# Attention and two feed-forward layers on one core: in the second pass, ready weight parts from DRAM, sums in place, and the next group's first unit ahead of each second stage

## The chip, the core and the metric

The kernel runs on one core of a Trainium2 chip. The metric is the device time of one execution in microseconds; the time before is the median of three runs, 1068.46 us (1065.6 to 1068.74).

## What is computed

Causal attention with a recurrent memory over 4 x 8 heads of 576 tokens and width 64; then two gated feed-forward layers on 2304 tokens of width 512. All of it is float32.

```python
...
    g = x @ w_gate
    silu = g * (1.0 / (1.0 + np.exp(-g)))
    val = x @ w_val
    return (silu * val @ w_out).astype(np.float32)
...
    h = x @ w_in
    g = h * (1.0 / (1.0 + np.exp(-1.702 * h)))
    return (g @ w_out).astype(np.float32)
```

The first layer has `d_ff` 1536, the second 2048. The weights come as 64-bit numbers and are decoded on the chip into float32, chunk by chunk (68 chunks of 128 x 512).

## The kernel before, in words

**Precision.** A float32 operand is split into a rounded high part (ScalarE casts it) and the rest as a low part (a subtraction on GpSimd or VectorE). A product is three matmuls: high by high, high by low, low by high.

**First pass.** Attention and both layers for the first 1024 tokens, a group of chunks at a time. Per chunk, `load_w` loads, `dec` decodes (ScalarE, VectorE, GpSimd), `spl0` (L160) and `spl1` (L163) make the two parts in the buffer `wp`, and 24 matmuls `m` of 512 columns use them. For the second pass `keep` (L176) stores the decoded float32 weights of two chunks (a pair) in a DRAM tile: for inner rows (the chunks of a `w_out`) four planes of 128 x 256, for the others seven, the last of them sums that `add_up` (L165) makes on GpSimd.

**Second pass.** The other 1280 tokens. Here each 2 x 2 block product of matrices is done with seven block products and not eight; the blocks are 640 columns wide. The names of the program:

- `P(l,g,k,j)`: product j of 0 to 6 in unit k of group g of layer l, the first stage (into the hidden rows). A unit is seven products; the first layer (l = 0) has three groups of four units, the second (l = 1) four groups of two.
- `Q(l,g,u,j)`: product j of half u in the second stage of a group (back to width 512): fourteen products. Q(l,g) below is such a stage.
- A product is 12 matmuls `c` of 320 columns; there are 238.
- Forms: the seven combinations of data blocks that the products take: `B11`, `B21`, `B22` are blocks, `T1` to `T4` differences of blocks (`t1` to `t4`, VectorE, L1072), each split by `hi` (ScalarE, L1088) and `lo` (L1093, VectorE, a few on GpSimd). For a Q they are made from its group's unit results (`f`), for a layer once from the layer's input (`xh`, `xl`, `th`, `tl`).
- In a unit: `s` copies product 0, `u` = s + product 2, `v` = u + product 3, `c22` = v + product 4, `u4` = u + product 4, `c21` = v + product 6, `c12` = u4 + product 5 (VectorE additions on PSUM, L1039); `tan2`, `gat2` and `mul` are the gate. Product 1 adds onto product 0 in PSUM. In a Q products 1, 5 and 6 do so onto 0, 4 and 3, after the sum `E` (L1110, VectorE) has read the bank.
- `E` adds a product into the output rows or into `csum`; `fin` (L1115) adds `csum` at a layer's end; `put` stores.
- Weights: `raw` (L976) loads a pair's planes, `add` (L984) makes four sums on GpSimd for inner rows, and for each product `wh` (ScalarE, L992) and `wl` (GpSimd, L996) split one plane into a buffer `wb`.

**What sets the order.** `schedule` plays a list schedule with given durations and keys; `pinned` emits each engine's instructions in that order, and an engine works its own list in order. `plan_three` writes the sequence of products: for each group all units, then its Q. Keys for forms come from tables (`SOON`, `THEN`), and tables of numbers (`SHARE`, `LEAD`) shift the first pass.

```python
            if l and g == 0 and WOVEN:
                todo = [(k, j) for j in OPEN for k in ks]
            else:
                todo = [(k, j) for k in ks for j in (LAST if g or not l or k else OPEN)]
...
            qs = [(u, j) for j in (CLOSE if close else SECOND) for u in range(2)]
```

The two units of group 0 of layer 1 are woven: each product of the one, then of the other.

Of the kernel before, what the change touches and what calls it, by code (L numbers as in the profile page):

```python
# [35 lines left out]
def tile_attention_moe_moe(  # L36
# [13 lines left out]
    nc = tc.nc  # L50
# [7 lines left out]
    const = ctx.enter_context(tc.tile_pool(name="const", bufs=1))  # L58
# [55 lines left out]
    kept = {i: dram.tile([128, 7 if first(i) else 4, 256], F32, name=f"w{i}") for i in range(0, NCK, 2)}  # L114
# [61 lines left out]
    def keep(i):  # L176
        a = raws[i].rearrange("p (a n) -> p a n", a=2)
        if not first(i):
            x = i % 2
            nc.sync.dma_start(out=kept[i - x][:, 2 * x:2 * x + 2], in_=a)  # L180
        elif i % 2 == 0:
            nc.sync.dma_start(out=kept[i][:, 0:2], in_=a)
        else:
            nc.sync.dma_start(out=kept[i - 1][:, 2:6], in_=sums.pop(i))
            nc.sync.dma_start(out=kept[i - 1][:, 6], in_=a[:, 1])
# [332 lines left out]
    PACE, DEC, SHARE, LEAD, XKEY = 2.93, 4.02, 0.879, 16.5, 60.16  # L518
# [54 lines left out]
    def decode_ops(ops, i, use, split=True, decode=True):  # L573
# [15 lines left out]
        if i % 2 == 0:
            ops["keep", i] = "SP", 0.4, need + 6.0, (("dec2", i),), (), ()  # L590
            return
        for x in range(2):
            ops["sum", i, x] = "Pool", 1.75, need + 5.0, (("spl1", i),) if x == 0 else (("sum", i, 0),), \
                ("sums",) if x == 0 else (), (("wa", ("dec0", i - 1)),) if x else ()
        ops["keep", i] = "SP", 0.8, need + 8.0, (("sum", i, 1),), (), (
            ("sums", ("sum", i, 0)), ("wa", ("dec0", i)))
# [39 lines left out]
    def plan_one():  # L636
# [12 lines left out]
    LATE = (("B11", 0), ("B22", 0), ("T3", 1), ("T4", 0))  # L649
    EV, WB, RAW = -2.5, 6.7, -10.3  # L650
    SOON = {
        "t1": 1.8, "t3": 5.2, "T3": -69.2, "t2": -31.2, "T2": 9.5, "B11": -15.2, "B21": 5.2, "T1": -15.6, "t4": -17.2,
        "T4": -11.8, "B22": -11.9}
    THEN = {
        "t1": -12.1, "t3": 6.5, "T3": 8.5, "t2": -1.6, "T2": 14.7, "B11": -17.8, "B21": 1.7, "T1": -11.5, "t4": 3.4,
        "T4": 16.0, "B22": 2.5}
    OPEN, CLOSE = (0, 1, 2, 3, 4, 6, 5), (0, 4, 1, 5, 3, 2, 6)
    WOVEN, HEAD = True, 3
# [34 lines left out]
    def form_ops(ops, G, b, key, to_f, from_t, late=(), early=False, wait=()):  # L693

        at_ = SOON if early else THEN

        def op(name, kd, after, takes=(), gives=()):
            ops[(name, G, kd)] = "DVE", 0.82, key + at_[name], tuple(after), takes, gives

        def split(F, kd, after, gives=()):  # L700
            after = (*after, *(wait if F[0] == "B" or F == "T1" else ()))
            ops["hi", G, F, kd] = "Act", 0.68, key + at_[F], after, ("f",) if to_f else (), ()
            e, us = ("Pool", 1.85) if (F, kd) in late else ("DVE", 0.82)
            ops["lo", G, F, kd] = e, us, key + at_[F], (("hi", G, F, kd),), (), tuple(gives)

        for kd in range(2):
# [16 lines left out]

# [3 lines left out]
    def plan_three(ops, t0, ready, gets):  # L727

        seq, n = [], 0
        for l, g in groups():  # L730
            base = 36 + 8 * g if l else 12 * g
            ks = (0, 2) if l else (0, 1, 2, 3)
            if l and g == 0 and WOVEN:
                todo = [(k, j) for j in OPEN for k in ks]
            else:
                todo = [(k, j) for k in ks for j in (LAST if g or not l or k else OPEN)]
            for k, j in todo:
                seq.append(("P", l, g, k, j))
                flat.append((base + (k if l else 2 * k), j))
            close = not l and g == 2  # L740
            qs = [(u, j) for j in (CLOSE if close else SECOND) for u in range(2)]
            if close and HEAD < 7:
                qs = qs[:2 * HEAD] + [(u, j) for u in range(2) for j in CLOSE[HEAD:]]
            for u, j in qs:
                seq.append(("Q", l, g, u, j))
                flat.append((base + (4 if l else 8) + 2 * u, j))
        left = {}
        for m, (i, j) in enumerate(flat):
            left[i] = m
        keys = [t0 + STEP * m for m in range(len(seq))]  # L750
        seen = set()
        for m, (i, j) in enumerate(flat):
            key = keys[m] - WB
            first = seq[m][0] == "P"
            if i not in seen:
                seen.add(i)
                ops["raw", i] = "SP", 2.2, key - RAW, (("seam", 1), *([("raw", was)] if m else gets)), ("raw",), ()
                was = i
                if not first:
                    for x in range(4):  # L760
                        ops["add", i, x] = "Pool", 0.88, key - 1.0, (("add", i, x - 1) if x else ("raw", i),), (), ()
            ops["wh", m] = "Act", 0.42, key, (
                ("raw", i) if first else ("add", i, 3), *([("wh", m - 1)] if m else [])), ("wb",), ()
            ops["wl", m] = "Pool", 0.9, key, (("wh", m),), (), (("raw", ("raw", i)),) if left[i] == m else ()
        start = {}
        for m, n in enumerate(seq):
            key, wb = keys[m], ("wb", ("wh", m))
            if n[0] == "P":
                _, l, g, k, j = n
                U = l, g, k  # L770
                after = [("wl", m), *ready[l][FORMS[j]], *seq[max(m - 1, 0):m]]
                if j == 1:
                    after.append(("s", *U))
                ops[n] = "PE", STEP, key, tuple(after), ("pc",) if j != 1 else (), (wb,)
# [5 lines left out]
                def P(j):  # L780
# [506 lines left out]
```

## Time and profile before

| what | value |
|---|---|
| median of three runs | 1068.46 us |
| the profiled execution | 1066.52 us, its span 1064.7 us |
| TensorE busy | 1004.1 us, 94% of the span |
| VectorE, GpSimd, ScalarE busy | 875.4, 804.4, 596.7 us |
| mean granted TensorE clock | 0.981 |
| data moved by DMA | 119.59 MB |

A row of the timeline is one or more instructions of one line in a row on one engine, with the idle time before them and what ended it. A row of a group gives its count, busy time and mean, and the idle time of the engine just before it. Consecutive matmuls overlap, so their pace is read from start to start, and a busy share of TensorE near 100% can hold slow matmuls. The granted clock is a share of 2.4 GHz.

### The profile page before, as it was taken

Reading aid. Unit: us, or ns where it says so; the run is one execution under the profiler, and the core shown is the slowest. Engines: PE = TensorE matmul, PEld = TensorE weight load, DVE = VectorE, ACT = ScalarE, POOL = GpSimd, SP = SyncE. Lnnn points to the kernel's source line nnn. Section 1 sums busy time; section 2 is a strip of 40 time slices with the busy share of each in tenths; the row PEclk is TensorE's granted clock in tenths of the full one; section 3 lists DMA queues with packets and bytes.
Section 4 is the critical chain, followed back from the end, with each engine's and each line's share of the span. In section 5 each row is a group of like instructions: output and inputs, shape, how many; then the busy total and the mean of one; then the engine's idle time right before and its main releaser. Section 6 shows DMA issues by size and latency. Waiting matters only on the chain.

```text
span 1064.7 us, 16958 instructions
## 1 busy us (share of the span) xinstructions
PE 1004.1 (94%) x5959; PEld 864.9 (81%) x5959; DVE 875.4 (82%) x1180; ACT 596.7 (56%) x1231; POOL 804.4 (76%) x808
## 2 busy tenths in 40 slices
PE   7998998999999999999999999999998689899896
PEld 4665776778787777777888999999997679799895
DVE  8999589777878977686889686697799996969797
ACT  6897466557465666755555455443444465535351
POOL 7879578886877767656564898797797787858685
PEclk9999999999999999999999999999999799999998
DMA  5362446564545434443544211203102103020202
GB/s 173 102 203 74 151 168 192 184 200 155 182 141 171 149 118 143 170 149 120 179 179 153 95 40 70 89 22 104 55 21 70 41 1 109 1 90 21 89 21 99
DMA packets 48932, 119.59 MB, mean 112 GB/s; under 512 B 7632, under 2 KB 14288, under 8 KB 48848
## 3 DMA queue, kind: packets, MB, share of 16 engines
q1 hardware_dynamic: 48704, 118.51, 33.5%
q8 instruction: 47, 0.77, 0.3%
q14 instruction: 37, 0.30, 0.1%
q10 hardware_dynamic: 144, 0.00, 0.0%
HBM read 85.46 MB, written 33.03 MB: 111 GB/s over the span
## 4 chain that ended last, share of the span: by engine, by line
PE 61%; DVE 27%; issue 4%; POOL 3%; ACT 3%; DMA 2%; SPq 0%; POOLq 0%; ACTq 0%; DVEq 0%
PE m L88 27%; PE c L88 24%; DVE t L1072 4%; PE o L88 4%; DVE f L1093 4%; PE s L88 3%; DVE t L1052 3%; DVE t L1039 2%; PE tp L361 2%; DVE acc L1110 2%; DVE nm L310 1%; DVE xl L1093 1%; DVE wa L146 1%; DVE sm L340 1%; DVE csum L1110 1%
## 5 line engine op out<-in xcount | busy, mean ns | idle before, releaser
L996 POOL TENSOR_TENSOR wb<-raw,wb 128x256 fp32r<-128x256 f32 x238 | 218.7, 940 | 62.3 <-ACT wb L992 61.0
L88 PE MATMUL c<-f,wb 128*128 128x320 f32 x1176 | 185.7, 319 | 26.6 <-DVE acc L1110 15.8
L88 PE MATMUL m<-xh,wp 128*128 128x512 f32 x640 | 210.3, 398 | 0.5 <-POOL wp L163 0.5
L88 PEld LDWEIGHTS c<-f,wb 128*128 128x128 f32 x1176 | 180.3, 195 | 31.1 <-DVE acc L1110 18.1
L88 PEld LDWEIGHTS m<-xh,wp 128*128 128x128 f32 x640 | 120.0, 188 | 35.0 <-issue 5.1
L88 PE MATMUL m<-hh,wp 128*128 128x512 f32 x448 | 147.6, 399 | 0.0
L149 POOL TENSOR_TENSOR wa<-wa,wr 128x512 uint32<-128x512 uint32 x68 | 95.7, 1409 | 65.3 <-DVE wa L146 48.3
L992 ACT CAST wb<-raw 128x256 fp32r<-128x256 f32 x238 | 89.6, 403 | 87.0 <-PE c L88 55.8
L163 POOL TENSOR_TENSOR wp<-wa,wp 128x512 fp32r<-128x512 f32 x68 | 95.1, 1398 | 55.8 <-ACT wp L160 55.0
L88 PE MATMUL c<-xh,wb 128*128 128x320 f32 x640 | 132.3, 312 | 4.4 <-ACT xh L1088 4.2
L1039 DVE TENSOR_TENSOR t<-t,c 128x640 f32<-128x640 f32 x120 | 95.4, 814 | 42.3 <-PE c L88 34.8
L88 PE MATMUL m<-xl,wp 128*128 128x512 f32 x320 | 124.7, 390 | 0.0
L1088 ACT CAST f<-t 128x640 fp32r<-128x640 f32 x98 | 71.2, 727 | 86.5 <-DVE t L1072 69.6
L88 PEld LDWEIGHTS c<-xh,wb 128*128 128x128 f32 x640 | 104.6, 191 | 5.1 <-ACT xh L1088 4.5
L88 PEld LDWEIGHTS m<-hh,wp 128*128 128x128 f32 x448 | 84.7, 189 | 21.2 <-issue 3.5
L88 PE MATMUL c<-th,wb 128*128 128x320 f32 x480 | 99.8, 311 | 0.3
L1072 DVE TENSOR_TENSOR t<-t,t 128x640 f32<-128x640 f32 x64 | 87.8, 1385 | 2.4 <-POOL t L1056 2.2
L88 PE MATMUL m<-hl,wp 128*128 128x512 f32 x224 | 87.8, 392 | 0.0
L349 POOL TENSOR_SCALAR p<-p,sm 128x256 f32<-128x256 f32 (+3 forms) x128 | 76.0, 611 | 13.7 <-DVE sm L341 5.2
L1093 DVE TENSOR_TENSOR f<-t,f 128x640 fp32r<-128x640 f32 x70 | 79.1, 1134 | 4.6 <-ACT f L1088 4.2
L88 PEld LDWEIGHTS c<-th,wb 128*128 128x128 f32 x480 | 78.2, 189 | 1.1 <-DVE t L1039 1.1
L88 PE MATMUL c<-xl,wb 128*128 128x320 f32 x320 | 73.9, 313 | 4.1 <-DVE xl L1093 4.1
(128 smaller groups left out, 2096.6 us busy)
## 6 DMA issues: line engine op xcount, KB each, us to landing
w<-w SPq DMA_DIRECT2D x40, 512.0 KB, 3.8
raw<-w SPq DMA_DIRECT2D x20, 896.0 KB, 4.6
w<-wo SPq DMA_DIRECT2D x28, 512.0 KB, 3.5
w<-wa SPq DMA_DIRECT2D x48, 256.0 KB, 3.3
w<-sums SPq DMA_DIRECT2D x20, 512.0 KB, 2.7
qk<-qk SPq DMA_DIRECT2D x32, 288.0 KB, 3.8
raw<-w SPq DMA_DIRECT2D x28, 256.0 KB, 3.0
nq<-nat SPq DMA_DIRECT2D x16, 320.0 KB, 3.8
```

Of the source, the lines that this page charges most:

```text
L88: nc.tensor.matmul(o, w, x, start=start, stop=stop, skip_group_check=more)
L149: nc.gpsimd.tensor_tensor(au, au, r, op=ALU.add)
L163: nc.gpsimd.tensor_sub(parts[i][:, 1], raws[i], f(parts[i][:, 0]))
L349: nc.gpsimd.tensor_scalar(p[:, j, c:c + n], p[:, j, c:c + n], sm[:, x, j:j + 1], 1.0, op0=ALU.mult, op1=ALU.mult)
L992: nc.scalar.copy(wb[:, 0], RAWS[i][:, j])
L996: nc.gpsimd.tensor_sub(WBS[m][:, 1], RAWS[i][:, j], f(WBS[m][:, 0]))
L1039: nc.vector.tensor_add(wide_(t), wide_(TT[(a, *U)]), pc("P", *U, j))
L1052: nc.vector.scalar_tensor_tensor(t, t, 1.0, c_in(n[:3], n[3]), op0=ALU.add, op1=ALU.mult)
L1072: nc.vector.tensor_sub(t, block(G, a, kd), block(G, b, kd))
L1088: nc.scalar.copy(form(G, F, kd)[0], block(G, SRC[F], kd))
L1093: e.tensor_sub(l, block(G, SRC[F], kd), f(h))
L1110: nc.vector.scalar_tensor_tensor(y, o, 0.5, y, op0=ALU.mult, op1=ALU.add)
```

## The change

- **Ready quarters.** For every pair the DRAM tile has ten planes. Planes 0 to 3 are the split parts (high and low) of the first chunk, stored from `wp`; planes 4 and 5 those of one quarter of the second; planes 6 to 9 what still is split in the second pass. There, products 0 and 1 take their weights straight from a load `da` (2 buffers), product 6 from a load `dz` (3 buffers); products 2 to 5 use `raw` (now four planes) with `wh` and `wl`. The buffers `wb` are 6 and not 8.
- **Sums in place.** In a unit, products 6 and 5 add onto products 3 and 4 in PSUM, after `v` and `c22`; `u4` is gone. `t1` and `t2` are written over their block. The order of a unit is 0, 2, 3, 4, 1, 6, 5 (it was 0, 2, 1, 3, 4, 6, 5).
- **The sequence.** Within a layer the first unit of the next group stands ahead of a group's Q. The last Q of a layer has none to put there.
- `fin` 0 and 1 move from GpSimd to VectorE, `fin` 2 to GpSimd. `schedule` gets a term for VectorE and GpSimd instructions that hold each other up; durations, keys and tables are new.

```diff
 def keep(i):
-        a = raws[i].rearrange("p (a n) -> p a n", a=2)
...
+        odd, to = i % 2, kept[i - i % 2]
+        w = f(parts[i])
+        if odd:
+            nc.sync.dma_start(out=to[:, 4:6], in_=w[:, :, 256:512])
+        else:
+            nc.sync.dma_start(out=to[:, 0:4], in_=w)
         if not first(i):
...
+            nc.sync.dma_start(out=to[:, 6 + 2 * odd:8 + 2 * odd], in_=raws[i].rearrange("p (a n) -> p a n", a=2))
+        elif odd:
+            nc.sync.dma_start(out=to[:, 6:10], in_=sums.pop(i))
...
+    SHARED = {"t1", "t2", "t3", "t4", "lo", "fin", "add", "wl", "mul", "gat2"}
...
+                        if n[0] in SHARED and (n[0] != "gat2" or n[-1]):
+                            t += OVER * max(0.0, hold.get("Pool" if e == "DVE" else "DVE", 0.0) - now)
+                            hold[e] = t
...
-    PACE, DEC, SHARE, LEAD, XKEY = 2.93, 4.02, 0.879, 16.5, 60.16
+    PACE, DEC, SHARE, LEAD, XKEY = 2.93, 4.02, 0.872, 16.9, 60.16
...
-    OPEN, CLOSE = (0, 1, 2, 3, 4, 6, 5), (0, 4, 1, 5, 3, 2, 6)
+    OPEN, CLOSE = (0, 1, 3, 2, 4, 6, 5), (0, 4, 1, 5, 3, 2, 6)
...
-    FIN = (("Pool", 1.85), ("Pool", 1.85), ("DVE", 0.82))
+    FIN = (("DVE", 0.74), ("DVE", 0.74), ("Pool", 1.53))
...
-    SECOND, LAST = (0, 4, 1, 5, 3, 2, 6), (0, 2, 1, 3, 4, 6, 5)
+    SECOND, LAST = (0, 4, 1, 5, 3, 2, 6), (0, 2, 3, 4, 1, 6, 5)
...
+            if DELAY and g:
+                items[-1:] = [*units[:DELAY], items[-1], *units[DELAY:], qs]
+            else:
+                items += [*units, qs]
...
+            part = "da" if j < 2 else "raw" if j < 6 else "dz"
...
+                if j in CHAIN:
+                    after.append(({1: "s", 6: "v", 5: "c22"}[j], *U))
...
-                    op("u4", "DVE", 0.82, (n, ("u", *U), ("c22", *U), ("v", *U)), (), (pc(4),))
...
+    def da(i):
+        t = DA[i] = cw.tile([128, 4, 256], F32R, tag="da", name="da")
+        nc.sync.dma_start(out=f(t), in_=kept[i][:, 0:4])
+
+    def dz(i):
+        t = DZ[i] = cw.tile([128, 2, 256], F32R, tag="dz", name="dz", bufs=3)
+        nc.sync.dma_start(out=f(t), in_=kept[i][:, 4:6])
...
+    def next_weight():
+        m = count["wb"]
+        count["wb"] += 1
         i, j = flat[m]
...
+        if j < 2:
+            return DA[i][:, j:4:2]
+        return DZ[i] if j == 6 else WBS.pop(m)
```

The order of the instructions is the scheduler's, so the diff does not show it. Three places follow.

VectorE, Q(1,1), from the second sum of product 0 on. `csum` and `acc` are `E`, `t<-t,t` are `t1` to `t4`, `f<-t,f` are `lo`. Before:

```order
L1110 SCALAR_TENSOR_TENSOR csum<-c,csum 128x640
L1110 SCALAR_TENSOR_TENSOR acc<-c,acc 128x640
L1072 TENSOR_TENSOR t_9277<-t_9443,t_9277 128x640
L1072 TENSOR_TENSOR t_9234<-t_9398,t_9234 128x640
L1072 TENSOR_TENSOR t_9528<-t_9443,t_9299 128x640
L1072 TENSOR_TENSOR t_9535<-t_9398,t_9319 128x640
L1110 SCALAR_TENSOR_TENSOR acc<-c,acc 128x640
L1093 TENSOR_TENSOR f_9514<-t_9277,f_9514 128x640
L1110 SCALAR_TENSOR_TENSOR acc<-c,acc 128x640 x3
L1093 TENSOR_TENSOR f_9538<-t_9528,f_9538 128x640
```
and of the change, from the first sum of product 0 on:

```order
L1151 SCALAR_TENSOR_TENSOR csum<-c,csum 128x640 x2
L1134 TENSOR_TENSOR f_9439<-t_9302,f_9439 128x640
L1151 SCALAR_TENSOR_TENSOR acc<-c,acc 128x640
L1113 TENSOR_TENSOR t_8810<-t_9302,t_8810 128x640
L1151 SCALAR_TENSOR_TENSOR acc<-c,acc 128x640
L1134 TENSOR_TENSOR f_9478<-t_8874,f_9478 128x640
L1113 TENSOR_TENSOR t_9248<-t_9248,t_8874 128x640
L1151 SCALAR_TENSOR_TENSOR acc<-c,acc 128x640 x2
L1134 TENSOR_TENSOR f_9481<-t_8810,f_9481 128x640
L1113 TENSOR_TENSOR t_9222<-t_9222,t_8810 128x640
```
Four differences stood in a row between the sums of products 0 and 4 and the next; now no two stand together, and sums stand between them.

VectorE, the end of Q(0,2) and the start of the second layer, from the last sum of product 2 (`csum<-c`) on; `acc<-acc,csum` is `fin`, `xl<-acc,xh` is `lo` of `B22` and `B21`, `acc<-acc` and `t<-acc,t` are `t3` and `t2`. Before:

```order
L1110 SCALAR_TENSOR_TENSOR csum<-c,csum 128x640
L1115 TENSOR_TENSOR acc<-acc,csum 128x640
L1093 TENSOR_TENSOR xl<-t_8498,xh 128x640
L1110 SCALAR_TENSOR_TENSOR acc<-c,acc 128x640
L1093 TENSOR_TENSOR xl<-acc,xh 128x640
L1072 TENSOR_TENSOR acc<-acc 128x640
L1093 TENSOR_TENSOR xl<-acc,xh 128x640
L1072 TENSOR_TENSOR t_8558<-acc,t_8447 128x640
L1072 TENSOR_TENSOR acc<-acc 128x640
L1072 TENSOR_TENSOR t_8567<-acc,t_8498 128x640
L1093 TENSOR_TENSOR xl<-acc,xh 128x640
```
and of the change:

```order
L1151 SCALAR_TENSOR_TENSOR csum<-c,csum 128x640
L1156 TENSOR_TENSOR acc<-acc,csum 128x640
L1151 SCALAR_TENSOR_TENSOR acc<-c,acc 128x640
L1156 TENSOR_TENSOR acc<-acc,csum 128x640
L1134 TENSOR_TENSOR xl<-acc,xh 128x640 x2
L1113 TENSOR_TENSOR acc<-acc 128x640 x2
L1134 TENSOR_TENSOR xl<-acc,xh 128x640
L1134 TENSOR_TENSOR tl<-acc,th 128x640
L1113 TENSOR_TENSOR acc<-acc 128x640
L1134 TENSOR_TENSOR xl<-acc,xh 128x640
```
After the last product's sum (`acc<-c,acc`) seven instructions ended with the `lo` of `B21`'s second half; now a `fin` and five end with it.

SP, the loads of Q(1,1) (pairs w_120 and w_121) and of what stands around it. Before:

```order
L981 DMA raw<-w_120 128x512
L982 DMA raw<-w_120 128x2x256
L981 DMA raw<-w_121 128x512
L982 DMA raw<-w_121 128x2x256
L979 DMA raw<-w_122 128x1792
L979 DMA raw<-w_123 128x1792
L981 DMA raw<-w_124 128x512
L982 DMA raw<-w_124 128x2x256
```
and of the change:

```order
L1005 DMA raw<-w_120 128x1024
L1013 DMA dz<-w_122 128x512
L1013 DMA dz<-w_120 128x512
L1005 DMA raw<-w_121 128x1024
L1009 DMA da<-w_120 128x1024
L1013 DMA dz<-w_121 128x512
L1009 DMA da<-w_121 128x1024
L1013 DMA dz<-w_123 128x512
L1005 DMA raw<-w_123 128x1024
L1009 DMA da<-w_123 128x1024
```
A pair's one or two loads have become three, and the loads of the next group's first unit (w_122) stand ahead of or among those of the Q.

## Rows read from the trace of the kernel before

**Rows 1.** Windows: length; busy us (count) of PE, PEld, DVE, ACT, POOL; clock; DMA share.

```profile
200.00:300.00 100.00, 100.00 (x516) 77.50 (x516) 74.59 (x117) 60.01 (x120) 76.78 (x79) 1.00 0.52 170
...
820.60:857.60 37.00, 28.55 (x171) 27.62 (x170) 35.81 (x38) 17.74 (x32) 26.65 (x22) 0.82 0.09 30
...
945.60:1058.30 112.70, 103.28 (x674) 101.38 (x672) 97.75 (x106) 50.69 (x97) 81.92 (x75) 0.97 0.14 48
```
**Rows 2.** Groups from 640 us on: TensorE, second stages.

```profile
L88 PE MATMUL c<-f,wb 128*128 128x320 f32 x1153 | 182.3, 319 | 26.6 <-DVE acc L1110 15.8 <-DVE f L1093 6.3 <-DVE csum L1110 3.0
```
**Rows 3.** Timeline of TensorE in the second pass: start, duration, instruction, count, idle before.

```profile
636.37 24.87 PE L88 MATMUL c<-f,wb 128*128 128x320 f32 x168
...
661.08 0.46 PE L88 MATMUL c<-xh,wb 128*128 128x320 f32 x2
...
710.45 8.38 PE L88 MATMUL c<-f,wb 128*128 128x320 f32 x56
...
737.75 0.46 PE L88 MATMUL c<-xh,wb 128*128 128x320 f32 x2
...
787.03 8.38 PE L88 MATMUL c<-f,wb 128*128 128x320 f32 x56
...
820.61 0.46 PE L88 MATMUL c<-xh,wb 128*128 128x320 f32 x2
...
829.83 0.90 PE L88 MATMUL c<-xh,wb 128*128 128x320 f32 x2 [4.22 <-ACT xh L1088]
...
857.57 1.34 PE L88 MATMUL c<-f,wb 128*128 128x320 f32 x8
...
889.25 0.45 PE L88 MATMUL c<-xh,wb 128*128 128x320 f32 x2
...
914.26 8.96 PE L88 MATMUL c<-f,wb 128*128 128x320 f32 x60
...
931.65 14.12 PE L88 MATMUL c<-f,wb 128*128 128x320 f32 x84 [3.63 <-DVE acc L1110]
...
945.61 0.46 PE L88 MATMUL c<-xh,wb 128*128 128x320 f32 x2
```
**Rows 4.** Two lines' and a tile's durations (ns min/median/max), then the timeline at 827 us.

```profile
L1072 DVE TENSOR_TENSOR t<-t,t x64: 810/1355/2189, 536.2 to 1049.7; 128x640 f32<-128x640 f32 x64
...
L996 POOL TENSOR_TENSOR wb<-raw,wb x238: 721/743/1976, 582.9 to 1043.9; 128x256 fp32r<-128x256 f32 x119
...
L1093 POOL TENSOR_TENSOR f<-t,f x28: 1566/1846/2149, 605.1 to 1049.9; 128x640 fp32r<-128x640 f32 x28
...
827.68 7.64 POOL L996 TENSOR_TENSOR wb<-raw,wb 128x256 fp32r<-128x256 f32 x6
...
830.85 1.34 DVE L1072 TENSOR_TENSOR acc<-acc 128x640 f32<-128x640 f32 x1
```
**Rows 5.** Groups of VectorE in the second pass.

```profile
L1039 DVE TENSOR_TENSOR t<-t,c 128x640 f32<-128x640 f32 x120 | 95.4, 814 | 42.3 <-PE c L88 34.8 <-ACT wb L992 6.3 <-POOL f L1093 0.5
...
L1072 DVE TENSOR_TENSOR t<-t,t 128x640 f32<-128x640 f32 x57 | 80.3, 1424 | 2.4 <-POOL t L1056 2.2
...
L1093 DVE TENSOR_TENSOR f<-t,f 128x640 fp32r<-128x640 f32 x70 | 79.1, 1134 | 4.6 <-ACT f L1088 4.2
```
**Rows 6.** Page: a group of the first pass, and a DMA issue to landing.

```profile
L88 PE MATMUL m<-xh,wp 128*128 128x512 f32 x640 | 210.3, 398 | 0.5 <-POOL wp L163 0.5
...
w<-w SPq DMA_DIRECT2D x40, 512.0 KB, 3.8
```
**Rows 7.** Timeline of GpSimd at the end.

```profile
1054.23 7.30 POOL L1115 TENSOR_TENSOR acc<-acc,csum 128x640 f32<-128x640 f32 x4 [2.31 <-DVE csum L1110]
```

More of the change, by code (lines that the diff above doesn't have):

```diff
@@ L112, in first @@
         return layer(i)[1] < layer(i)[2]
-    kept = {i: dram.tile([128, 7 if first(i) else 4, 256], F32, name=f"w{i}") for i in range(0, NCK, 2)}
+    kept = {i: dram.tile([128, 10, 256], F32, name=f"w{i}") for i in range(0, NCK, 2)}
     bits, raws, parts, sums, stages = {}, {}, {}, {}, {}
@@ L585, in decode_ops @@
         _, at_, ins, _ = layer(i)
+        odd = i % 2
         if at_ >= ins:
-            ops["keep", i] = "SP", 0.4, need + 2.0, (("spl1", i),), (), (("wa", ("dec0", i)),)
+            ops["keep", i] = "SP", 0.8 if odd else 1.2, need + 2.0, (("spl1", i),), (), (("wa", ("dec0", i)),)
             return
[L589 to L596, printed above, removed]
+        if odd:
+            for x in range(2):
+                ops["sum", i, x] = "Pool", 1.75, need + 5.0, (("spl1", i),) if x == 0 else (("sum", i, 0),), \
+                    ("sums",) if x == 0 else (), tuple(("wa", ("dec0", n)) for n in (i - 1, i)) if x else ()
+        ops["keep", i] = "SP", 1.2 if odd else 0.8, need + 6.0, (("sum", i, 1) if odd else ("spl1", i),), (), (
+            (("sums", ("sum", i, 0)),) if odd else ())
     def unit_ops(ops, i, c, key, ends, bank, lead=2.0):
@@ L727, in plan_three @@
     def plan_three(ops, t0, ready, gets):
-        seq, n = [], 0
+        seq, items = [], []
         for l, g in groups():
-            base = 36 + 8 * g if l else 12 * g
             ks = (0, 2) if l else (0, 1, 2, 3)
             if l and g == 0 and WOVEN:
-                todo = [(k, j) for j in OPEN for k in ks]
+                units = [[(k, j) for j in OPEN for k in ks]]
             else:
[L736 to L746, printed above, removed]
@@ L747, in plan_three @@
-        left = {}
+                units = [[(k, j) for j in (LAST if g or not l or k else OPEN)] for k in ks]
+            units = [[("P", l, g, *x) for x in unit] for unit in units]
+            order = CLOSE if not l and g == 2 else SECOND
+            head = HEAD if not l and g == 2 else TAIL if l and g == 3 else 7
+            qs = [("Q", l, g, u, j) for j in order[:head] for u in range(2)]
+            qs += [("Q", l, g, u, j) for u in range(2) for j in order[head:]]
+            if DELAY and g:
+                items[-1:] = [*units[:DELAY], items[-1], *units[DELAY:], qs]
+            else:
+                items += [*units, qs]
@@ L748, in plan_three @@
+        seq = [n for item in items for n in item]
+        for kind, l, g, x, j in seq:
+            base = 36 + 8 * g if l else 12 * g
+            flat.append((base + ((x if l else 2 * x) if kind == "P" else (4 if l else 8) + 2 * x), j))
+        wh, loads, ends = None, [], {}
         for m, (i, j) in enumerate(flat):
-            left[i] = m
+            ends[i, "da" if j < 2 else "raw" if j < 6 else "dz"] = m
         keys = [t0 + STEP * m for m in range(len(seq))]
-        seen = set()
         for m, (i, j) in enumerate(flat):
[L753 to L759, printed above, removed]
-                    for x in range(4):
[L761 to L764, printed above, removed]
@@ new lines, in plan_three @@
+            part = "da" if j < 2 else "raw" if j < 6 else "dz"
+            key = keys[m] - (WB if part == "raw" else 0.0)
+            new = seq[m][0] == "P"
+            if (part, i) not in ops:
+                ops[part, i] = "SP", 0.55 if part == "dz" else 1.1, key - (RAW if part == "raw" else DIR), (
+                    ("seam", 1), *gets), (part,), ()
+                if part == "raw" and not new:
+                    for x in range(4):
+                        ops["add", i, x] = "Pool", 0.7, key - 1.0, (("add", i, x - 1) if x else ("raw", i),), (), ()
@@ L765, in plan_three @@
+            if part == "raw":
+                ops["wh", m] = "Act", 0.32, key, (
+                    ("raw", i) if new else ("add", i, 3), *([("wh", wh)] if wh is not None else [])), ("wb",), ()
+                ops["wl", m] = "Pool", 0.7, key, (("wh", m),), (), (("raw", ("raw", i)),) if ends[i, "raw"] == m else ()
+                wh = m
         start = {}
         for m, n in enumerate(seq):
-            key, wb = keys[m], ("wb", ("wh", m))
+            i, j = flat[m]
+            part = "da" if j < 2 else "raw" if j < 6 else "dz"
@@ L768, in plan_three @@
+            key, ready_w = keys[m], (part, i)
+            wb = ()
+            if part == "raw":
+                wb, ready_w = (("wb", ("wh", m)),), ("wl", m)
+            elif ends[i, part] == m:
+                wb = ((part, (part, i)),)
             if n[0] == "P":
@@ L770, in plan_three @@
                 U = l, g, k
[L771 to L774, printed above, removed]
+                after = [ready_w, *ready[l][FORMS[j]], *seq[max(m - 1, 0):m]]
+                if j in CHAIN:
+                    after.append(({1: "s", 6: "v", 5: "c22"}[j], *U))
+                ops[n] = "PE", STEP, key, tuple(after), ("pc",) if j not in CHAIN else (), wb
                 ev = key - EV
```

166 lines of the change are left out of this document (84 added, 82 removed).

## The prediction

> **What bounds the kernel now.** I read the windows first. From 200 to 300 us TensorE is busy all the time, and that lasts to the end of the first pass [rows 1]; nothing that the change does to the other engines there can pay. In the second pass it is not: in the last 113 us it is busy for 103, at a mean granted clock of 0.97, and in the first unit of the second layer for 28.6 of 37.0 us, at 0.82. So the second pass holds what can be won. The groups from 640 us on say who is waited for: TensorE idles 26.6 us before products of the second stages (`c<-f`), 25.1 of them for VectorE's `acc`, `f` and `csum` [rows 2].
>
> The timeline of TensorE tells where [rows 3]. The 14 products of the first second stage, Q(0,0), have no wait: from 636.37 to the next unit at 661.08 are 24.71 us, 1.765 us a product. Against these 24.71 us, 14 products elsewhere take: Q(0,1) 710.45 to 737.75, 27.30, so 2.6 lost; Q(0,2) 787.03 to 820.61, 33.58, 8.9 lost; the two woven units that open layer two, 820.61 to 857.57, 36.96, 12.3 lost (a wait of 4.22 us for `xh`, which is ScalarE's, behind VectorE, and after it a pair of matmuls in 0.90 us and not 0.46, at 1.2 GHz, the lower of the clock's two levels); Q(1,0) 857.57 to 889.25, 31.68, 7.0 lost; Q(1,1) 914.26 to 945.61, 31.35, 6.6 lost, and Q(1,2) and Q(1,3) repeat it to 0.2 us. In all 2.6 + 8.9 + 12.3 + 7.0 + 3 x 6.6 = 50.6 us. In the units between, almost nothing is lost.
>
> Why VectorE is late: a subtraction of two SBUF tiles takes it 0.81 us at best and 1.355 in the median [rows 4], and it is the long value that goes with a busy GpSimd: at 827 to 835 us six GpSimd subtractions of 0.74 us take 7.64 us, 1.27 each, and VectorE's beside them 1.34 each. In the second pass the two largest groups (57 and 70 of them, means 1.424 and 1.134) cost 57 x 0.61 + 70 x 0.32 = 57 us more than at 0.81 [rows 5].
>
> **The change, part by part.**
>
> *Ready quarters.* Of seven weight splits per pair of chunks, three go: 34 x 3 = 102 ScalarE casts (off the path) and 102 GpSimd subtractions of 0.743 us in the median [rows 4], 76 us of GpSimd. GpSimd is nobody's direct cause in rows 2; its gain is VectorE's. I take VectorE's loss to shrink with GpSimd's work beside it. In a group of layer two GpSimd now has 28 splits, 8 sums and 4 low parts (36 x 0.74 + 4 x 1.6 = 33 us, both at their shortest [rows 4]), then 16, 8 and 4: 24 us.
>
> Here the Trainium skill is to be weighed. Its page "SBUF — State Buffer", section "Who interferes with whom", says that a VectorE instruction with two SBUF inputs and a GpSimd instruction that reads SBUF exclude each other for the whole instruction, the later one being blocked. The alternating stretch of rows 4 agrees that they exclude each other, but not for whole durations: a pair advances in 1.27 us, not in 0.81 + 0.74 = 1.55. What that rule would make of the sum is the first rival below.
>
> *The price: transfers.* A pair's kept data grows from 7 (or 4) planes of 128 KB to 10, so 34 x 10 - (20 x 7 + 14 x 4) = 144 planes, 18.9 MB, more written in the first pass and read in the second. Over 587 us that is 32 GB/s, on 170 GB/s at a share of 0.52 [rows 1]: a share near 0.62. I take nothing for it: TensorE waits for a split weight 0.5 us in 640 matmuls [rows 6], and a part's buffer is needed again only four chunks later. A chunk has 24 matmuls and 100 us hold 516 [rows 1], so that is 18 us, against a landing of some 4 us [rows 6]. In the second pass the quarters go into 2 and 3 buffers with no engine between. The tightest is the quarter for the second product of a Q: its buffer is freed by the fifth product of the unit ahead, three products (5.3 us) before it is wanted; 512 KB land in 3.8 us. Margin 1.5 us: nothing, with an upper bound of 2 us for each of seven Qs (3.8 to a landing of 7).
>
> *Sums in place.* `u4` goes: 20 VectorE additions, 0.81 us each, 16 us, and the sixth and seventh products of a unit now add onto the third's and fourth's PSUM. So they wait for `v` and `c22`, issued two products, 3.5 us, earlier. VectorE's additions on PSUM idle 34.8 us for TensorE [rows 5]; on the whole VectorE is ahead there, and I take zero. Above it lies the second rival.
>
> *The next group's first unit ahead of each Q.* It gives the forms of a Q 7 x 1.765 = 12.4 us more, in Q(0,0), Q(0,1), Q(1,0), Q(1,1), Q(1,2). The unit's loads, splits and sums move ahead with it on SP, GpSimd and VectorE: what they cost is in the lists counted here. From 945.6 to 1058.3 us VectorE does 106 instructions in 97.8 us [rows 1]; at 0.74 from start to start they are 78, so 19 us are contention in two groups. With 24/33 of it and 6 instructions fewer: 100 x 0.74 + 14 = 88 us for 2 x 28 products = 98.8 us. It fits, if it isn't bunched, and now it isn't: the wait of 3.63 us in Q(1,1) [rows 3] is for the `E` that stands behind four `t` in a row; in the new order no two `t` stand together. So Q(0,1) keeps 0.3 of 2.6, Q(1,0) 0.5 of 7.0, Q(1,1) and Q(1,2) 0.5 of 6.6 each: 2.3 + 6.5 + 12.2 = **21.0 us won**; the worst I allow is half.
>
> *Q(1,3)* has no next unit to be put ahead of it. But its unit for the first two blocks is done before Q(1,2), so `B11` and `T1` are ready, and the forms of the late blocks come in by 10 to 18 us, when I count VectorE's list at 0.75 us for a sum and 1.0 for a shared one, against 10.6 to 21 us when wanted. Keeps 1.5: **5.1 won**.
>
> *Q(0,2)*, the end of layer one, also gets nothing ahead. VectorE's list from its first `E` to the last: 31 instructions before, 14 sums of PSUM and 17 shared ones. The new list to the last `fin` has 30, 14 and 16, since two `fin` come from GpSimd to VectorE for each half. Before, these 31 fill the 33.6 us of the stage: 10.8 us of them contention (31 x 0.735 = 22.8). GpSimd has 14 splits and 6 long ones beside it, 20 us; then 8 and 5, 14 us. So 30 x 0.735 + 10.8 x 14/20 = 29.6 us, from some 5 us after the stage's start. The last chained product waits for the `E` of the same half's third form, 25th of the 30, at 5 + 25/30 x 29.6 = 29.7; with itself, 31.4 against 24.7. Keeps 6.4 of 8.9: **2.5 won**.
>
> *The opening of layer two.* What is late is `lo(B21,1)`. Before, its chain went through a `fin` on GpSimd of 2 us and seven VectorE subtractions at 1.34 [rows 4]. Now the `fin` is VectorE's, five subtractions follow it, and only the other `fin`, two splits and a low part stand on GpSimd beside them. From the end of Q: `E` and `fin` 2.0, five of 0.8 to 1.1, so 6.0 to 7.5; wanted at two products and a half, 4.7. Wait 1.3 to 2.8; then `T3` (five more against 3.8 us) 0.2 to 1.9, `T2` 0.5 to 1.0, and as much as 1.5 at 1.2 GHz. I take 5.0 of 12.3: **7.3 won**, bounds 4 to 10.
>
> *The tail.* Four `fin` in a row on GpSimd end 1061.53, 3.2 us before the end [rows 7]. Now two of the six are GpSimd's and start earlier; the last, on VectorE, ends some 2.2 us behind the last product: **0.5 won**. Of the hand-over from the first pass, where four stores of outputs now stand ahead of the last kept chunk on SP, I take 0.5 us as lost.
>
> Sum: 21.0 + 5.1 + 2.5 + 7.3 + 0.5 - 0.5 = 35.9. The profiled execution took 1066.5 (span 1064.7): 1030.6, say **1031 us**. The median of the three runs, 1068.46, lies 1.9 above that execution, the lowest 0.9 below; I let that widen the range and not move the number.
>
> **The rivals.**
>
> *The port was the bound.* If the exclusion of rows 4 holds all the time, the work of both engines on it must be added. Counted in the program: on GpSimd 238 splits at 0.743, 56 sums at 0.74 and 60 long ones at 1.6, on VectorE some 195 instructions with two SBUF inputs at 0.81; 177 + 41 + 96 + 158 = 472 us. The second pass has 238 x 1.765 = 420 us of products and 51 lost: 471. Then 76 us less leave TensorE alone as the bound, and all of the 50.6 goes but the opening's own dependence, some 3 us: 1066.5 - 48 = 1018. This is the result that the Trainium skill's rule gives, as on the page named. Against it: a pair takes 1.27 us and not 1.55, so the sum is nearer 390 and the port free a sixth of the time. For it: how close the numbers are. 0.15.
>
> *The chained products wait instead.* Where VectorE runs late, the sixth product of a unit now stops TensorE until `v` is out, and the seventh until `c22`; before, both took free banks. 3.5 us of lag is free; behind it every microsecond counts, in 20 units. At 1.8 us a unit the 36 us are spent and the time is that of before; at 2.5 us it is 1066.5 + 14 = 1080, slower. For it: a lag of 3 to 5 us is what rows 3 show in every Q, and now the next unit's products stand next to them. Against it: that lag is in the second half of Qs, where the unit is not. 0.04 for slower, 0.03 for the same.
>
> *Half of it.* The bunch only moves: the longer list of a group spills into the unit behind, and the three middle Qs of layer two and Q(1,3) keep half, 13 us and not 3, with the seam as it was, 21 and not 11.4. Then 1066.5 - 36 + 10 + 9.6 = 1050. 0.14.
>
> **How the numbers follow.** The forecast has 0.64, with a range of its own of 1022 to 1041 from the bounds named. The range of eight in ten takes in the port's rival (1018, and 2 below for it) and most of the half: 1016 to 1049. About 0.3% can be told from no change here. All cases but the chained wait are faster by far more: faster 0.93, same 0.03, slower 0.04.
>
> **What would show it.** 136 splits on GpSimd; VectorE's `t` and `f` subtractions with a mean near 1.1 and not 1.13 to 1.42; Q(1,0) to Q(1,2) in 25 to 26 us; the opening of layer two in 28 to 32 us; no wait over 1 us in the units. Wrong would be: waits for `v` or `c22` in the units, `da` landings that end a wait of TensorE, or a first pass that ends after 590 us.

## The result and the profile after

The changed kernel takes **1020.1 us** (median of four runs, 1018.65 to 1022.13) against 1068.06 of the kernel before (median of four): a ratio of 0.956, 95% interval 0.953 to 0.958. The forecast was 1031 with a range of 1016 to 1049: faster, inside the range, and 11 us better than the point.

The profiled execution took 1020.71 us, its span 1018.9. Windows, with the columns of [rows 1]: of the change, the same stretch of the first pass and the second pass from its first product to its last; then the second pass of the kernel before.

```profile
200.00:300.00 100.00, 100.00 (x517) 78.17 (x516) 82.76 (x120) 60.14 (x124) 76.79 (x79) 1.00 0.61 207
584.90:1013.70 428.80, 421.43 (x2857) 418.67 (x2855) 350.48 (x389) 190.31 (x340) 271.62 (x247) 1.00 0.34 107
```
```profile
587.10:1058.50 471.40, 435.93 (x2857) 429.33 (x2855) 391.75 (x410) 223.05 (x439) 377.86 (x349) 0.97 0.16 55
```

The second pass is 42.6 us shorter. TensorE's idle time went from 35.5 to 7.4 us, which is 28.1 of them; the other 14.5 are busy time, 435.9 against 421.4 us for the same products: the granted clock was 0.97 and is 1.00. VectorE lost 41 us of work, GpSimd 106.

How much of the 14.5 us is the clock can be estimated. Before, the clock was 1.2 GHz in six stretches of the second pass, 30.7 us in all, and TensorE was busy for 23.7 us of them. Its timeline in one of them:

```profile
835.49 1.27 PE L88 MATMUL c<-xh,wb 128*128 128x320 f32 x4
836.55 0.73 PE L88 MATMUL c<-xl,wb 128*128 128x320 f32 x2
```

Four matmuls start in 1.06 us there, and 12 in 1.76 us, four in 0.59, at 2.4 GHz. So of the 23.7 us of busy time some 11 are the lower clock. Where the other 3 to 4 us went was not followed up; 1.1 of them are in the first stages of layer two's last three groups, which took 25.0 us each and now take 24.6.

Timeline of TensorE, second pass, the columns of [rows 3]. The stages Q(0,1) and Q(1,0), each from its first row to the first of the unit behind it, and, between them, Q(0,2) and the opening of layer two:

```profile
721.55 3.68 PE L89 MATMUL c<-f,da 128*128 128x320 f32 x24
...
742.67 3.68 PE L89 MATMUL c<-f,dz 128*128 128x320 f32 x24
746.20 0.46 PE L89 MATMUL c<-xh,da 128*128 128x320 f32 x2
...
783.13 3.68 PE L89 MATMUL c<-f,da 128*128 128x320 f32 x24
...
798.80 0.85 PE L89 MATMUL c<-f,wb 128*128 128x320 f32 x4 [0.26 <-DVE f L1134]
800.81 1.45 PE L89 MATMUL c<-f,dz 128*128 128x320 f32 x8 [1.16 <-DVE acc L1151]
802.96 0.85 PE L89 MATMUL c<-f,dz 128*128 128x320 f32 x4 [0.70 <-POOL f L1134]
...
810.83 2.03 PE L89 MATMUL c<-f,dz 128*128 128x320 f32 x12 [1.74 <-DVE acc L1151]
812.70 0.46 PE L89 MATMUL c<-xh,da 128*128 128x320 f32 x2
...
818.95 0.57 PE L89 MATMUL c<-xl,da 128*128 128x320 f32 x2 [1.39 <-DVE xl L1134]
...
840.93 0.46 PE L89 MATMUL c<-xh,da 128*128 128x320 f32 x2
...
853.25 3.68 PE L89 MATMUL c<-f,da 128*128 128x320 f32 x24
...
874.37 3.68 PE L89 MATMUL c<-f,dz 128*128 128x320 f32 x24
877.89 0.46 PE L89 MATMUL c<-xh,da 128*128 128x320 f32 x2
```

Q(0,1) and Q(1,0) take 24.64 us each, which is 14 products at 1.76 us, with no wait; Q(1,1), Q(1,2) and Q(1,3) repeat that. Waits are left at two places, in Q(0,2) and in the opening of layer two, and one of 0.98 us in the very first unit. Stage by stage, in us won:

| stage | before | after | won | forecast |
|---|---|---|---|---|
| Q(0,1), Q(1,0), Q(1,1), Q(1,2) | 121.5 | 98.6 | 22.9 | 21.0 |
| Q(1,3) | 31.4 | 24.6 | 6.7 | 5.1 |
| Q(0,2) | 33.6 | 29.6 | 4.0 | 2.5 |
| opening of layer two | 37.0 | 28.2 | 8.7 | 7.3 |
| other products | 247.8 | 247.7 | 0.1 | 0 |
| behind the last product | 6.4 | 5.4 | 1.0 | 0.5 |
| ahead of the second pass | 587.1 | 584.9 | 2.2 | -0.5 |
| sum (won: of the spans; the parts are rounded) | 1064.7 | 1018.9 | 45.8 | 35.9 |

The groups of VectorE and GpSimd from 640 us on, to be held against [rows 2] and [rows 5], with TensorE's products of the second stages:

```profile
L89 PE MATMUL c<-f,wb 128*128 128x320 f32 x672 | 101.3, 309 | 0.3 <-DVE f L1134 0.3
L89 PE MATMUL c<-f,da 128*128 128x320 f32 x336 | 51.6, 309 | 0.0
L89 PE MATMUL c<-f,dz 128*128 128x320 f32 x168 | 26.4, 311 | 3.6 <-DVE acc L1151 2.9 <-POOL f L1134 0.7
L1029 POOL TENSOR_TENSOR wb<-raw,wb 128x256 fp32r<-128x256 f32 x115 | 105.1, 924 | 72.8 <-ACT wb L1026 71.0 <-PE c L89 0.9 <-POOL wb L1029 0.8
L1134 DVE TENSOR_TENSOR f<-t,f 128x640 fp32r<-128x640 f32 x64 | 69.5, 1089 | 8.1 <-ACT f L1129 7.8
L1113 DVE TENSOR_TENSOR t<-t,t 128x640 f32<-128x640 f32 x52 | 59.9, 1160 | 0.8 <-POOL t L1095 0.3
```

The idle 26.6 us before second-stage products are 3.9. VectorE's two kinds of subtraction average 1.16 and 1.09 us, against 1.42 and 1.13 in [rows 5]; at 52 and 64 of them that is 16 us of VectorE's time, so the 42 us did not come from shorter subtractions alone.

### The profile page after: what moved, and what is told of

Same layout as the page of the kernel before. It is cut to its first block, busy times and chain, and to the rows that moved or that the text cites. A ratio compares the mean times of both kernels' runs of the same rounds, so it can differ in the third digit from the quotient of the medians.

```text
span 1018.9 us, 16779 instructions
## 1 busy us (share of the span) xinstructions
PE 991.2 (97%) x5959; PEld 854.7 (84%) x5959; DVE 838.0 (82%) x1163; ACT 562.8 (55%) x1129; POOL 696.8 (68%) x703
## 4 chain that ended last, share of the span: by engine, by line
PE 79%; DVE 17%; issue 1%; DMA 1%; ACT 1%; POOL 0%; SPq 0%; ACTq 0%; DVEq 0%
PE c L89 36%; PE m L89 31%; PE o L89 5%; PE s L89 3%; PE tp L363 2%; DVE nm L312 2%; DVE hl L968 1%; DVE phi L256 1%; DVE s L310 1%; DVE tl L1134 1%; DVE t L1113 1%; DVE acc L1151 1%; DVE wa L146 1%; DVE acc L1113 1%; DVE wa L147 1%
## 5 line engine op out<-in xcount | busy, mean ns | idle before, releaser
L1029 POOL TENSOR_TENSOR wb<-raw,wb 128x256 fp32r<-128x256 f32 x136 | 123.5, 919 | 86.9 <-ACT wb L1026 84.2
L1026 ACT CAST wb<-raw 128x256 fp32r<-128x256 f32 x136 | 53.2, 405 | 108.4 <-PE c L89 95.0
L89 PEld LDWEIGHTS m<-hh,wp 128*128 128x128 f32 x448 | 83.9, 188 | 23.7 <-issue 3.8
L89 PE MATMUL c<-f,wb 128*128 128x320 f32 x672 | 101.3, 309 | 0.3 <-DVE f L1134 0.3
L89 PEld LDWEIGHTS c<-f,wb 128*128 128x128 f32 x672 | 99.2, 188 | 0.5 <-DVE f L1134 0.5
L326 ACT ACTIVATE p<-s,nm 128x256 f32<-128x256 f32 (+3 forms) x128 | 66.1, 530 | 29.4 <-DVE nm L312 24.4
L1134 POOL TENSOR_TENSOR f<-t,f 128x640 fp32r<-128x640 f32 x28 | 50.4, 1801 | 39.9 <-ACT f L1129 39.8
L1113 DVE TENSOR_TENSOR t<-t,t 128x640 f32<-128x640 f32 x64 | 73.2, 1150 | 1.7 <-POOL t L1095 1.0
L89 PEld LDWEIGHTS m<-xl,wp 128*128 128x128 f32 x320 | 60.2, 188 | 11.6
L161 ACT CAST wp<-wa 128x512 fp32r<-128x512 f32 x68 | 42.3, 621 | 50.0 <-POOL wa L150 19.8
L147 DVE SCALAR_TENSOR_TENSOR wa<-w,wa 128x512 uint32<-128x512 uint32 x68 | 65.7, 965 | 2.3
```

The costliest lines, as they stand in the source:

```text
L89: nc.tensor.matmul(o, w, x, start=start, stop=stop, skip_group_check=more)
L147: nc.vector.scalar_tensor_tensor(au, top, 0xC0000000, au, op0=ALU.bitwise_and, op1=ALU.bitwise_or)
L326: nc.scalar.activation(p[:, j, c:c + n], s[:, j, c:c + n], AF.Exp, bias=nm[:, x, j:j + 1], accum_out=sm[:, x, j:j + 1])
L1026: nc.scalar.copy(wb[:, 0], weight(m))
L1029: nc.gpsimd.tensor_sub(WBS[m][:, 1], weight(m), f(WBS[m][:, 0]))
L1113: nc.vector.tensor_sub(t, block(G, a, kd), block(G, b, kd))
```

## The experiments

Three readings stood against each other: the prediction's own sum, by place; the rival "The port was the bound", whose 1018 us the result came close to; and, later, a third: that what counts is the time in GpSimd's own list. All kernels below are the changed one with an edit, except for one. Times are medians of four runs; single runs of a kernel differ by 1 to 5 us, so a difference of 1 us is none. The experiments ran on four chips, and the kernel before, beside them, had medians of 1065.7 to 1067.5 us (1068.1 above); between chips even 2 us say little. Where an edit changes the list of operations, the planner lays out a new order. What a stage loses is its time in the profile over 1.765 us a product; in the changed kernel Q(0,2) loses 4.9 us, the opening 3.5, the first unit 1.0, and the rest nothing.

**1. The move undone.**

```diff
-    WOVEN, HEAD, TAIL, DELAY = True, 3, 6, 1
+    WOVEN, HEAD, TAIL, DELAY = True, 3, 6, 0
```

> The changed kernel with DELAY = 0: every Q stands directly behind its own units again, all else of the change stays (the planner lays the order out anew). By the prediction's sum the move carried most of the 21 us of Q(0,1), Q(1,0), Q(1,1), Q(1,2); without it each of them keeps some 0.7 of its old loss, as the prediction's own scaling for Q(0,2) gave (6.4 of 8.9): 1.9 + 5.0 + 4.7 + 4.7 = 16 us, so about 1036. By the theory of the port (the work of VectorE and GpSimd on two SBUF inputs adds up, and 76 us less of it leave TensorE as the bound) the place of the Qs is worth little: 1020 to 1024.

Measured: 1031.8 us, 11.7 more. In the profile Q(1,0) loses 8.3 us again, Q(1,1) and Q(1,2) 1.1 each, Q(0,1) and Q(1,3) nothing. So the move is worth 11.7 us here, and that nearly all in one stage; the others are mended without it.

**2. GpSimd's work put back.**

```diff
...
+            elif wh is not None:
+                ops["ex", m] = "Pool", 0.7, key - WB, (("wl", wh),), (), ()
...
+    def ex(m):
+        s = spare[0]
+        nc.gpsimd.tensor_sub(s, f(s), f(s))
```

> The changed kernel with one subtraction of 128x256 on GpSimd more for each of the 102 products whose weights now come ready: it works on a spare tile, nothing waits for it, and it stands in GpSimd's order where the next split weight is made. The order of the products, the loads and the sums in place stay. By the prediction's sum only the contention comes back in its old share (33 to 24): 1.5 us each in the Qs with a unit ahead, 1.5 in Q(1,3), 2.5 in Q(0,2), 4 in the opening: about 1032. By the theory of the port the whole 45 us come back: 1058 to 1064.

Measured: 1030.0 us, 9.9 more. The port's rival falls: it wanted 1058 to 1064. The loss is where the prediction had it: the opening loses 8.1 us (4.6 more than in the changed kernel) and Q(0,2) 5.9 (1.0 more), but the Qs behind it only 2.5 together.

**3. Both.**

> The changed kernel with DELAY = 0 and the 102 GpSimd subtractions on the spare tile together: of the change there stay the loads, the sums in place, and fin on VectorE. By the prediction's sum 16 and 12 us come back, and some more as the two meet in the Qs: 1048 to 1055. By the theory of the port the same as with the subtractions alone, 1058 to 1064.

Measured: 1046.2 us, 26.1 more, where the two alone give 21.6. All Qs but Q(0,0) lose again, 1.2 to 8.6 us. Without the move's 12 us of room the late list shows.

**4. and 5. Is it contention, or GpSimd's time?** The subtraction on the spare tile is replaced by memsets, which read nothing from SBUF: three of 256 columns with an order of their own; then, in exactly the orders of experiment 2,

```diff
-        nc.gpsimd.tensor_sub(s, f(s), f(s))
+        for n in (256, 256, 128):
+            nc.gpsimd.memset(f(s)[:, :n], 0.0)
```

> The changed kernel with three memsets of 128x256 on GpSimd for each of the 102 products with ready weights: GpSimd is held at least as long as by a subtraction each (a memset of 128x128 takes 0.204 us in the trace), but reads nothing from SBUF. By the theory of the port, and by the prediction's sum, the time stays at 1020 to 1023, and VectorE's t and f subtractions keep their means of 1.16 and 1.09 us. If it is GpSimd's own lateness (its splits, sums and low parts coming later) that the removed splits had caused, the time rises as much as with the subtractions on the spare tile.

> The kernel with the 102 extra subtractions, in exactly its orders on every engine, but each subtraction on the spare tile replaced by memsets of 256, 256 and 128 columns: GpSimd is held as long (0.31 + 0.31 + 0.20 = 0.83 us by the memset rows of the run before, 0.81 for the subtraction) and reads nothing. The run before with memsets was planned anew and lost 9.8 us in one place, so it did not settle this. If the extra subtractions cost what they did by holding up VectorE, the 10 us go again: 1020 to 1023. If it was by making GpSimd's own splits, sums and low parts later, the time stays at 1029 to 1031.

Measured: 1034.0 us for the first, with one wait of 5.85 us in Q(1,0) that its new order made; it settles nothing. The second took 1029.95 us, the same as experiment 2. The second passes of experiment 2, then of this one (columns of [rows 1]):

```profile
585.90:1023.00 437.10, 425.05 (x2857) 420.88 (x2855) 363.46 (x388) 191.47 (x340) 356.34 (x348) 0.99 0.33 104
```
```profile
586.00:1023.40 437.40, 426.06 (x2857) 423.05 (x2855) 354.65 (x388) 191.02 (x340) 349.24 (x550) 0.98 0.33 104
```

VectorE is 8.8 us less busy for the same 388 instructions, and the pass is no shorter. So the extra subtractions did not cost their 10 us by holding VectorE up.

**6. The move alone**, in the kernel before:

```diff
...
+            if g:
+                items[-1:] = [units[0], items[-1], *units[1:], qs]
+            else:
+                items += [*units, qs]
```

> The kernel before with the sequence of the change alone: the first unit of the next group ahead of each Q; weights, sums, fin and keys as before, the order planned anew. The two runs with the extra subtractions, with and without the move, differ by 16 us. If the move is worth that by itself, the time is 1048 to 1053. If it pays only where GpSimd and VectorE have been relieved, since the unit's own splits and sums move ahead with it into the same stretch, it is worth under 5 us here: 1062 to 1072.

Measured: 1045.5 us against 1067.3 for the kernel before beside it: 21.8 us won by the sequence of the products alone, with the order laid out for it, a little more than expected. Q(0,1), Q(1,0), Q(1,1) and Q(1,2) lose under 2 us together. The opening keeps 11.6, Q(0,2) 6.5, Q(1,3) 3.7, and the unit ahead of Q(1,0) now loses 5.3 us: TensorE waits there for VectorE's sums `t` (2.49 us the longest), and a stretch at 1.2 GHz follows.

**7. and 8. A sum back; `fin` back.**

```diff
...
+                    op("u4", "DVE", 0.74, (("c21", *U), ("c22", *U)), (), (pc(4),))
...
-                    op("c12", "DVE", 0.74, (n, ("u", *U), ("c21", *U)), (), (pc(4),))
+                    op("c12", "DVE", 0.74, (n, ("u4", *U)), (), (pc(5),))
```
```diff
-    FIN = (("DVE", 0.74), ("DVE", 0.74), ("Pool", 1.53))
+    FIN = (("Pool", 1.53), ("Pool", 1.53), ("DVE", 0.74))
```

> The changed kernel with product 5 of a unit in a bank of its own again: u4 (VectorE, 0.81 us) is back in each of the 20 units, and the product no longer waits for c22. The prediction took the sums in place at zero: 1019 to 1022. If VectorE's time is short in this kernel (350 of 428 us busy in the second pass), 16 us more of it come back in the Qs and the opening: 1025 to 1032.

> The changed kernel with fin 0 and 1 on GpSimd and fin 2 on VectorE, as before. By the prediction the opening of layer two gained most of its 8.8 us by this move, so it loses 4 to 6 of them again, and the tail 0.5: 1024 to 1027. If the opening gained by fewer subtractions on GpSimd beside it, the place of fin is worth under 1.5 us: 1020 to 1022.

Measured: 1024.2 us with the sum, 4.1 more, between the two expectations. Not the units but the opening loses most again, 7.3 us, while Q(0,2) loses only 2.1; experiment 9 below loses as much in the opening by its order alone, so what is the sum here and what the new order is not shown. With `fin` back 1021.0, which can't be told from the change; in the profile the opening loses 6.4 and not 3.5 us, and Q(0,2) 0.7 less.

**9. and 10. Order or time?** Experiment 2 changed two things, GpSimd's work and the planner's order. First its order with the subtractions left out (`ex` does nothing); then the changed kernel's own order with a subtraction put behind `wl`:

```diff
...
     names = schedule(ops, at)
+    names = [x for n in names for x in (n, *behind.get(n, ()))]
```

> Exactly the orders of the kernel with the 102 extra subtractions, on every engine, but those subtractions are left out: GpSimd has the work of the changed kernel, in an order that the planner laid out for more. If the extra subtractions cost their 10 us by the time that they take in GpSimd's list, the time is that of the changed kernel, 1019 to 1023. If it was the order, which the planner lays out otherwise with them, it stays at 1028 to 1031.

> The reverse: the changed kernel's orders on every engine, with a subtraction on the spare tile put behind GpSimd's split before each product with ready weights (100 of them), without planning anew. By GpSimd's time, 1028 to 1036, a little more than with the order planned for it. If it was the order, 1019 to 1022.

Measured: 1025.0 and 1031.8 us. Of the 9.9 us of experiment 2, 4.9 are the order (its opening loses 8.1 us with the work and 7.9 without), and 5.0 the work. In the old order the work costs 11.7, with 10.3 us lost in Q(0,2) and 3.5 in Q(1,0), against 4.9 and none in the changed kernel. How it gets to TensorE can be followed at the start of Q(0,2). `t<-t,t` on GpSimd is `mul`, the last product of the gate in layer one. GpSimd in experiment 10 (L1101 is `mul`, L1029 and L1035 are splits and extra work), then in the changed kernel (L1095 is `mul`):

```profile
787.77 1.19 POOL L1035 TENSOR_TENSOR spare<-spare 128x256 fp32r<-128x256 f32 x1
788.92 1.31 POOL L1029 TENSOR_TENSOR wb<-raw,wb 128x256 fp32r<-128x256 f32 x1
790.20 3.03 POOL L1101 TENSOR_TENSOR t<-t,t 128x640 f32<-128x640 f32 x2
```
```profile
784.59 1.57 POOL L1095 TENSOR_TENSOR t<-t,t 128x640 f32<-128x640 f32 x1
788.40 2.09 POOL L1095 TENSOR_TENSOR t<-t,t 128x640 f32<-128x640 f32 x1 [2.23 <-DVE t L1091]
```

VectorE and TensorE in experiment 10 around it:

```profile
784.35 1.73 DVE L1084 TENSOR_TENSOR t<-t,c 128x640 f32<-128x640 f32 x2
...
788.41 1.23 DVE L1097 SCALAR_TENSOR_TENSOR t<-t,t 128x640 f32<-128x640 f32 x1
792.52 1.39 DVE L1140 TENSOR_TENSOR f<-t,f 128x640 fp32r<-128x640 f32 x1 [2.88 <-ACT f L1135]
793.84 1.54 DVE L1157 SCALAR_TENSOR_TENSOR csum<-c,csum 128x640 f32<-128x640 f32 x2
```
```profile
794.71 5.32 PE L89 MATMUL c<-f,da 128*128 128x320 f32 x24 [4.04 <-DVE csum L1157]
```

In the changed kernel the two `mul` start at 784.59, right behind a split, and at 788.40, as soon as VectorE delivers. In experiment 10 VectorE has done what the first needs by 786.1 us and the second by 789.6 (the last of the gate, L1097), but splits, extra subtractions and a low part stand ahead of them in GpSimd's list: the first starts at 790.20 and the second right behind it. ScalarE's cast waits for the first block, VectorE's `lo` for the cast (2.88 us idle), the two sums `csum` stand behind that `lo` on VectorE, and TensorE, whose next product adds onto their bank, waits 4.04 us for them. GpSimd appears in no wait of TensorE's here; it is three links back.

**11. All four back**: experiments 1, 2, 7 and 8 together.

> The changed kernel without the move, with the 102 subtractions on GpSimd, with u4 and product 5 in its own bank, and with fin as before: of the change there stay the loads, without 102 casts on ScalarE, product 6 in product 3's bank, and the planner's durations, keys and its term for VectorE and GpSimd. If u4 and fin are worth what they were alone (4 and 1 us), 1050 to 1053, and what is left to the kernel before is the planner's order and the casts. If those two carry more where the Qs stand behind their units, 1058 to 1066.

Measured: 1060.6 us, 7 below the kernel before (ratio 0.993, interval 0.992 to 0.995). Q(1,1), Q(1,2) and Q(1,3) lose 6.5 us each again, as before. From experiment 3 on, the sum and `fin` cost 14.4 us, not the 5 that they cost under the move. What the last 7 us come from (no casts, product 6 in place, new keys) was not taken apart.

**12. Contention, in the old order**: experiment 10 with the memsets of experiment 5.

> The changed kernel's orders with memsets of 256, 256 and 128 columns in place of the 100 subtractions of the run before last (which took 1031.8 us). If what those cost was VectorE being held up, most of the 11.7 us go: 1020 to 1024. If it was the time in GpSimd's list, as the two runs with the planner's own order say (both 1029.95), the time stays at 1029 to 1033, with VectorE's t and f subtractions nearer the 1.19 and 1.10 us of the changed kernel than the 1.30 and 1.21 with the subtractions.

Measured: 1029.0 us, 2.8 less than with the subtractions and 8.9 more than without. Part of the 2.8 may be the chip's: the kernel before took 1065.66 us beside this run and 1067.53 beside experiment 10. The second passes of experiment 10, then of this one:

```profile
585.20:1024.30 439.10, 424.11 (x2857) 420.22 (x2855) 367.23 (x388) 189.77 (x340) 355.00 (x348) 1.00 0.32 103
```
```profile
585.50:1021.10 435.60, 423.94 (x2857) 420.28 (x2855) 349.90 (x389) 189.96 (x340) 345.62 (x550) 1.00 0.32 104
```

VectorE's 17 us of contention are gone (350 as in the change), most of the cost is not. The same two `mul` stand back to back, at 790.56.

The costs of undoing, side by side: move 11.7, splits 9.9, sum 4.1, `fin` 0.9, added up 26.6; all four at once 40.5. Each of these kernels has an order of its own, and only for the splits was the order taken apart from the work. No kernel of these beats the change.

## Why the prediction was right, and where its steps failed

**What bounds the kernel, and where: right.** The losses stood in the stages named, and the gain came out of these stages one by one; in each of them the forecast was low, by 1.4 to 1.9 us. The last 99 us were to need 88 us of VectorE; in 915.0 to 1013.5 us it was busy for 89.2.

**The move (21.0): right in size, and it can bring that alone** (experiment 6: 21.0 in its four stages, 3.0 in Q(1,3) and 3.1 at the end of layer one and the opening, with 5.3 given back in the moved unit). But the sum gave it the middle Qs as its own, and in the changed kernel undoing it costs 11.7, the new order included. The parts overlap: what the Qs needed was their forms some microseconds earlier, and the move, the splits and the sums each give some.

**What the stages keep (1.8 in the four Qs, 1.5, 6.4 and 5.0): too much.** Measured were 0, 0, 4.9 and 3.5. The term that failed is the rest that I left in stages with a covered list: five of the six Qs lose nothing. It is not that waits became shorter there; they went, and with them the lower clock. Before, 1.2 GHz stretches began in the second pass at 803, 827, 868, 933, 988 and 1046 us, each in or right behind a wait of 1.9 to 4.2 us; after, where the longest wait is 1.74 us, there is none in it. That is most of the 14.5 us of busy time above; the losses of the sum held them, and the rests assumed kept a part. Three slips in the sums stand beside this: 31.4 against 24.7 in Q(0,2) is 6.7 and not 6.4; two and a half products are 4.4 us and not 4.7; five instructions of 1.1 against 3.8 us are late by 1.7 and not 1.9. The first alone touches the forecast, by 0.3 us.

**"GpSimd is nobody's direct cause in rows 2; its gain is VectorE's": wrong.** I scaled VectorE's contention with GpSimd's work. Experiments 5 and 12 take the contention of the extra work away and get 0.0 and at most 2.8 us back of 9.9 and 11.7. GpSimd's work costs by its place in GpSimd's list, through `mul`, casts and low parts, and 4.9 us of experiment 2 were the order that was laid out for it.

The memsets agree with what the Trainium skill states on its page "SBUF — State Buffer", section "Who interferes with whom": a VectorE instruction with two SBUF inputs contends with a GpSimd instruction that reads SBUF, not with one that only writes it. Here 388 or 389 VectorE instructions took 367.2 us beside the subtractions, 349.9 beside the memsets, and 350.5 with neither.

**The sums in place (0): right only under cover.** One of them back costs 4.1 us, its new order included, and together with `fin` 14.4 where the Qs stand directly behind their units. TensorE waits for VectorE's sums `t` 1.9 us in three places, none of them ahead of a product 5 or 6: the chained wait did not come. They stand ahead of a product 3 in the first unit and of both products 4 in the opening, where the kernel before has no wait for VectorE's `t`; the sum had no such waits, and what makes them was not tried.

**The transfers (0): right.** No wait of TensorE's in the second pass ends on a load, `da` lands in 4.2 us, and the DMA share in the first pass is 0.61, forecast 0.62.

**`fin` and the opening (7.3): right in size, 8.7; the reason is mixed.** Of the waits counted, the one for `lo(B21,1)` came, 1.39 us against 1.3 to 2.8; for `T3` and `T2` none is over 0.2 us. `fin` back loses 2.9 of the 8.7 in the profile, the splits back 4.6, and 4.4 of those without any work, by the order.

**The hand-over (-0.5): wrong sign.** The second pass begins 2.2 us earlier. In the twelve profiles with the changed first pass it begins at 582.5 to 586.3 us, in the two others at 587.1 and 589.5; why was not tried.

**The rivals.** The port's 1018 is nearer to the result than the forecast, and its mechanism is refuted by 28 us in experiment 2: a right number is no proof. "Half of it" did not come either.

## What to carry to other kernels

An engine that ends no wait of the bottleneck can still be the cause two or three queues back: follow the late instruction's input through each engine's list. Parts of a change that relieve the same wait are not additive; undo each alone and all together (here 26.6 against 40.5 us, with new orders in each). And where a planner sets the order, run the new order without the new work before giving the work its cost: in experiment 2 half of it was order.

## What was not expected of the hardware

GpSimd work that reads SBUF and work that only writes it cost the same time in one order (experiments 2 and 5), and 11.7 against 8.9 us in the other (10 and 12), though VectorE was 9 and 17 us busier beside the first: contention on an engine with slack in the right places was nearly free here. And with the longer waits gone the granted clock stayed at 1.00 through the second pass, which by the estimate above gave some 11 of the 42.6 us there.
